# Relative-bias attention with a sine MLP on one core: the bias factors from matmuls instead of a pass through DRAM, and the first batch's values as casting loads

## The chip, the core and the metric

The kernel runs on one core of a Trainium2 chip. The core has a matrix engine (TensorE, PE in the profile, its weight loads PEld), a vector engine (VectorE, DVE), an engine for functions such as exp and sin (ScalarE, ACT), a general one (GpSimd, POOL) and one that mostly issues DMAs (SyncE, SP). Each has its own instruction stream and they meet through semaphores. SP, ACT and POOL can put loads into DMA queues; POOL's queue is called software_dynamic in the profile, that of SP and ACT hardware_dynamic. A load that changes the type from f32 to f16 on its way is called a casting load here; all of them are on POOL's queue. The metric is the time of one execution on the device in microseconds (us): before the change 375.01 us, the median of three runs (374.7 to 375.42).

## What is computed

Eight batches of attention with eight heads, 576 positions and head size 64, with a bias that depends on the distance of two positions alone; then an MLP on all 4608 rows with h + sin(alpha h)^2 / alpha as its function.

```python
scores = scale * np.matmul(q, k.transpose(0, 1, 3, 2))
bias = bias_table[bucket]                # bucket of |i - j|, 32 of them
scores = scores + bias.transpose(2, 0, 1)[None, :, :, :]
attn = np.exp(scores - np.max(scores, axis=-1, keepdims=True))
attn = attn / (np.sum(attn, axis=-1, keepdims=True) + 1e-09)
x = np.matmul(attn, v)                   # then to rows of 512
h = x @ w_in                             # 512 to 2048
s = np.sin(alpha * h)
out = (h + s * s / (alpha + 1e-09)) @ w_out
```

Buckets of all distances of 128 and more are the last one. The kernel uses exp(score + bias) = exp(score) times a factor, with the last bucket's bias taken off everywhere: the factor is then 1 outside a band of distances, and only blocks of the score matrix near the diagonal have to be multiplied. That band of factors, 384 wide for each head, is the tile `m2r` (with `mhr`, a smaller one for the last 64 keys of each head) before the change.

## The kernel before

**Stages.** For each batch t: keys and queries are brought to `kT` and `qT` (head dimension on partitions); TensorE makes scores for one pair of heads and 128 keys at a time (`qk` in `plan_unit`, kind A; kind C are the last 64 keys); ACT takes exp of them from PSUM into `u` (line 723); DVE multiplies by the band (lines 754 and 740); TensorE multiplies by the values `vs` and `vhs`, whose extra column of ones gives the row sum; DVE divides (lines 967, 968); the result goes to `xT`. Then come 16 steps f of the first MLP matmul, each with ACT's sin (1083), a square on ACT or DVE (1090, 1092) and DVE's sum (1097); the second MLP matmul (`w_out`) fills gaps of the next batch's attention.

**The first batch.** Its keys and queries come as plain or casting loads (`nat0` inside the tile natx, `nat1`), are cast on DVE and ACT (lines 488, 539, 540) and transposed on TensorE (`plan_tr`, lines 573 and 579); DVE copies the result to `kT` and `qT` (562). Its values come in f32 through SP's queue into a part of the `w_out16` tile (`load_v32`) and POOL casts them (`cast_v`). The band is made in `plan_table`: a small matmul takes the last bucket off the table, exp, a matmul with a constant 0/1 matrix phi spreads it over distances, ACT copies the 8 x 512 result to `e_sb`, which is written to DRAM (`e_dram`), and loads with one row's shift per partition read it back into `m2r` and `mhr`.

**The order of the work.** The instructions in the file's straight part (clears, first loads, seven matmuls on the zero tile `zz`) are issued in that order. All others are tasks of a planner (`Plan`), which simulates the five engines with the costs that each task names, picks the task that can start first (ties by priority), and emits the instructions in that order; `nb` is an earliest start that the code names for a task, and `HEAD_PRI` replaces the priority of some tasks by number. On each engine the chip then runs them in exactly that order. Where TensorE would have nothing to do in the first part, the planner puts in matmuls on `zz`. Waits are not written by hand: a layer below records what each instruction reads and writes, tile by tile, and makes the later instruction wait for the earlier one. POOL's loads take eight semaphores in turn.

**Lines that the text names.** `clear` (469 to 475) sets the parts of `kts`, `vhs` and `vs` that loads don't write, among them the column of ones of `vs` (475); for the first of two buffers it is called with DVE ahead of all casts, for the second with POOL.

Of the kernel before, what the change touches and what calls it, by code (L numbers as in the profile page):

```python
# [34 lines left out]
LAT = {"PE": 0.2, "ACT": 0.18, "DVE": 0.18, "POOL": 0.2, "SP": 2.4}  # L35
NBUF = {"ut": 2, "u": 2, "g": 2, "s16": 3, "sq": 3, "outs": 5, "xn": 6}
PAIRS = ((0, 1), (2, 3), (4, 5))
BANKS = {"h": (0, 1, 2, 3, 4, 5), "av": (6, 7), "mo": (7, 6)}

# [21 lines left out]
class Plan:  # L61
# [86 lines left out]
    def run(self, t0):  # L148
        free = dict(t0)
        todo = list(self.tasks)  # L150
        while todo:
# [21 lines left out]
            for e, c in cands.items():  # L173
                if not c:
                    continue
                s0 = min(x[0] for x in c)
                st, t = min(((x[0], x[1]) for x in c if x[0] <= s0 + SLACK[e]),
                            key=lambda x: (x[1].pri, x[0]))
                fin = st + t.engs[e]
                if best is None or (st, fin) < best[:2]:  # L180
                    best = (st, fin, e, t)
# [32 lines left out]
T_START = {"PE": 4.25, "ACT": 5.2, "DVE": 5.05, "POOL": 5.5, "SP": 5.0}  # L214
SPLIT = {0: 3, 1: 3}
PRI_S = 0
T_WI = 16.4
T_TAB = 4.9
T_PHI = 5.4
T_CL = 9.6  # L220
T_FIRST = (4.3, 5.35)
T_PAIR = ((7.05, 8.1), (8.9, 10.6), (12.5, 13.4))
PRI_TR = (350, 950, 1250)
T_VT = 9.7
T_ACT = ()
T_M2 = (12.4, 14.6, 16.0, 16.0)
T_MH = 13.5
T_RST = 20.0
T_WL = 25.0
T_V0 = (6.5, 8.8, 16.4, 16.9, 17.4, 17.9, 18.4, 18.9)  # L230
T_P3 = 8.3
# [5 lines left out]
T_LD = 33.0  # L237
# [4 lines left out]
SQ = {"ACT": 0.52, "DVE": 0.38}  # L242
T_V = ((15.0, 15.0), (53.5, 53.5))
T_TR1 = (35.5, 39.0)
T_W = (24.2, 27.0, 33.0, 33.0)
T_WO = (42.0, 45.0, 47.8, 51.0)
WARM0 = 7
WARM1 = 0
# [18 lines left out]
}  # L267
SIN_SET = "trig_and_small"
SLACK = {"PE": 0.02, "ACT": 0.02, "DVE": 0.02, "POOL": 0.02, "SP": 0.02}
# [14 lines left out]
def kernel(  # L284
# [26 lines left out]
    NE = 5  # L311
# [8 lines left out]
    e_dram = nc.dram_tensor("e_dram", [NE, 4 * H, EW], F16, kind="Internal")  # L320

    bt = _bucket_table(256)
    phi_np = np.zeros((NB, EW), dtype=np.float16)
    for x in range(EW - 1):
        phi_np[bt[abs(x - 255)], x] = 1.0
    last_np = np.eye(NB, dtype=np.float32)
    last_np[NB - 1] -= 1.0
    phi_h = nc.inline_tensor(phi_np, "phi_const")
    last_h = nc.inline_tensor(last_np, "last_const")
# [8 lines left out]
    m2r = sgl.tile([128, H, XW], F16, name="m2r")  # L338
    mhr = sgl.tile([128, NP, 192], F16, name="mhr")
    m2 = m2r[:, :, ::-1]  # L340
    mh = mhr[:, :, ::-1]
# [3 lines left out]
    vst = w_out16.rearrange("p f n -> p (f n)")[:, 0 : 2 * H * 4 * D].bitcast(F32).rearrange(  # L345
        "p (h c d) -> p h c d", h=H, c=4)
    vtt = w_out16.rearrange("p f n -> p (f n)")[:, 2 * H * 4 * D : 2 * H * 4 * D + 2 * NP * D].bitcast(
        F32).rearrange("p (h d) -> p h d", h=NP)
# [6 lines left out]
    tabE = sgl.tile([NB, H], F16, name="tabE")  # L355
    phi_sb = sgl.tile([NB, EW], F16, name="phi_sb")
    less_last = sgl.tile([NB, NB], F32, name="less_last")
    e_sb = sgl.tile([H, EW], F16, name="e_sb")
    alphaN = sgl.tile([NF, 128], F32, name="alphaN")
    idf_sb = sgl.tile([NF, NF], F32, name="idf_sb")  # L360
# [43 lines left out]

    def stage_kq(t):
        for dst, src in ((staged_k, k), (staged_q, q)):
            nc.gpsimd.dma_start(
                out=dst.ap()[t].rearrange("s (h d) -> s h d", h=H),
                in_=src[t].rearrange("h s d -> s h d"),
            )  # L410

    def load_kqT(t):
        nc.sync.dma_start_transpose(out=kTs[t % 2][:, :, :], in_=staged_k.ap()[t])
        nc.sync.dma_start_transpose(out=qTs[t % 2][:, :, :], in_=staged_q.ap()[t])

    def load_kt(t):
        for z in range(2):
            r = slice(64 * z, 64 * z + 64)
            nc.gpsimd.tensor_copy(out=kts[t % 2][r, :, r], in_=kTs[t % 2][r, :, 512:S])  # L419

    def load_v16(t):
        vp = v[t].rearrange("h s d -> s h d")
        for c in range(4):
            nc.gpsimd.dma_start(  # L424
                out=vs[t % 2][:, c, :, 0:D], in_=vp[128 * c : 128 * c + 128],
            )
        for z in range(2):
            load_vt(t, z)

    def load_v32(h):  # L430
        nc.sync.dma_start(out=vst[:, h], in_=v[0, h, 0:512].rearrange("(c p) d -> p c d", p=128))

    def load_vt32():
        vq = v[0].rearrange("(hp two) s d -> two s hp d", two=2)
        for z in range(2):
            nc.sync.dma_start(out=vtt[64 * z : 64 * z + 64], in_=vq[z, 512:S])

    def cast_vt():
        for z in range(2):
            r = slice(64 * z, 64 * z + 64)  # L440
            nc.gpsimd.tensor_copy(out=vhs[0][r, :, VC * z : VC * z + D], in_=vtt[r])

    def cast_v(h):
        nc.gpsimd.tensor_copy(out=vs[0][:, :, h, 0:D], in_=vst[:, h])
# [16 lines left out]
    def load_w_out16():  # L461
        src = moe_w_out.rearrange("(f p) n -> p f n", p=128)
        for fh in range(4):
            nc.gpsimd.dma_start(
                out=w_out16[:, 4 * fh : 4 * fh + 4, :], in_=src[:, 4 * fh : 4 * fh + 4, :]
            )

    def clear(eng, i):
        eng.memset(kts[i][0:64, :, 64:128], 0.0)
        eng.memset(kts[i][64:128, :, 0:64], 0.0)  # L470
        eng.memset(vhs[i][0:64, :, VC : 2 * VC], 0.0)
# [20 lines left out]
    def load_m2r(eng, h0, h1, r):  # L492

        eng.dma_start(
            out=m2r[:, h0:h1],
            in_=bass.AP(tensor=e_dram, offset=EW * (4 * H * r + h0), ap=[[1, 128], [EW, h1 - h0], [1, XW]]),
        )

    def load_mhr(eng):
        for z in range(2):  # L500
            eng.dma_start(  # L501
                out=mhr[64 * z : 64 * z + 64],
# [43 lines left out]
    def loads3():  # L546
        load_v16(1)
# [699 lines left out]
```

## Time and profile before

| | |
|---|---|
| median of three runs | 375.01 us |
| span of the profiled execution, first to last instruction | 372.5 us |
| what lies around the span, against the median | 2.5 us |
| busy share of PE, ACT, DVE, POOL | 98%, 85%, 69%, 24% |
| first cast of keys on DVE starts | 4.01 us |
| first exp on ACT starts | 9.39 us |
| first MLP matmul starts | 29.67 us |
| last idle time of PE over 0.3 us in the first 60 us ends | 52.40 us |

The page names lines of the kernel before. A row of the timeline is: start, time to the end of the last instruction of the row, engine, line, operation, tiles written and read, shape, count, and in brackets the engine's idle time before it with what ended it. A row of the windows is: stretch, its length, then busy time and count for PE, PEld, DVE, ACT and POOL, then the granted clock of TensorE, the DMA share and GB/s.

### The profile page before, as it was taken

The numbers are of one execution on the slowest core, as the hardware profiler recorded it, in microseconds if no ns is written. First come the engines' busy times: TensorE is split into PE (matmuls) and PEld (weight loads), VectorE is DVE, ScalarE is ACT, GpSimd is POOL, SyncE is SP. The second block draws the span as 40 slices with busy tenths as digits, with TensorE's granted clock in tenths as the row PEclk, the third lists the DMA queues.
The fourth block names the chain that finished last, engine by engine and source line by source line (L and its number), as shares of the span: only waits on it lengthen the run. The fifth ranks groups of instructions, "written<-read, shape, count | busy, mean of one in ns | idle before, by whom it ended". The sixth has DMA issues, their size and how long they took to land.

```text
span 372.5 us, 8907 instructions
## 1 busy us (share of the span) xinstructions
PE 363.7 (98%) x3563; PEld 195.3 (52%) x3563; DVE 258.8 (69%) x555; ACT 318.3 (85%) x436; POOL 89.2 (24%) x130
## 2 busy tenths in 40 slices
PE   6989989999999999999999999999999999999996
PEld 2455445644465445784554456444676455444443
DVE  4697966678776967597659866787669675879100
ACT  2898999989998999799989999899979997999211
POOL 5575360065000730064003700090006000000000
PEclk9599999999999999999999999999999999999999
DMA  9799999299824996199917992699249121000122
GB/s 167 152 191 208 203 170 155 61 146 123 113 60 99 115 151 112 48 161 138 135 48 135 126 169 59 115 114 171 60 111 118 65 58 48 7 18 13 59 85 84
DMA packets 149690, 40.69 MB, mean 109 GB/s; under 512 B 137144, under 2 KB 144656, under 8 KB 149648
## 3 DMA queue, kind: packets, MB, share of 16 engines
q0 software_dynamic: 94928, 17.47, 58.1%
q1 hardware_dynamic: 54352, 22.30, 25.5%
q8 instruction: 28, 0.46, 0.5%
q10 hardware_dynamic: 368, 0.34, 0.3%
q14 instruction: 14, 0.11, 0.1%
HBM read 37.73 MB, written 16.56 MB: 146 GB/s over the span
## 4 chain that ended last, share of the span: by engine, by line
PE 87%; DVE 4%; DMA 3%; ACT 3%; issue 1%; SPq 0%; ACTq 0%; DVEq 0%
PE pb L478 86%; DVE g L1097 1%; DMA tabN<-in_bias_table_dram 1%; DVE u L754 1%; DMA m2r<-e_dram 1%; DMA e_dram<-e_sb 1%; ACT sq L1090 1%; PE pb L1039 1%; ACT s L1083 1%; ACT nat L723 1%; DVE sq L1092 0%; DVE kT L562 0%; ACT L1161 0%; SPq L501 0%; DVE xn L968 0%
## 5 line engine op out<-in xcount | busy, mean ns | idle before, releaser
L723 ACT ACTIVATE u<-pb 128x1024 f16<-128x1024 f32 (+1 forms) x146 | 137.6, 1015 | 8.8 <-PE pb L478 7.4
L478 PE MATMUL pb<-w_out,g 128*128 128x512 f16 (+2 forms) x592 | 138.7, 374 | 0.5 <-DVE kT L562 0.5
L478 PE MATMUL pb<-xT,w_in 128*128 128x512 f16 (+4 forms) x704 | 127.5, 340 | 0.0
L1097 DVE SCALAR_TENSOR_TENSOR g<-sq,inv_a,pb 128x512 f16<-128x512 f16 x144 | 101.1, 743 | 7.7 <-ACT sq L1090 3.8
L1083 ACT ACTIVATE s<-pb,alphaT 128x512 f16<-128x512 f32 x144 | 92.9, 692 | 11.1 <-PE pb L478 10.2
L478 PEld LDWEIGHTS <-w_in 128*128 128x128 f16 x704 | 64.6, 98 | 57.1
L754 DVE TENSOR_TENSOR u<-u,m2r 128x768 f16<-128x768 f16 (+1 forms) x128 | 63.2, 498 | 35.6 <-ACT u L723 33.7
L478 PEld LDWEIGHTS <-g 128*128 128x128 f16 x592 | 54.0, 98 | 60.3 <-issue 5.4
L478 PEld LDWEIGHTS <-u 128*128 128x128 f16 x1152 | 43.1, 97 | 10.9 <-issue 5.8
L1090 ACT ACTIVATE sq<-s 128x512 f16<-128x512 f16 x75 | 46.8, 637 | 1.2 <-DVE g L1097 0.3
L419 POOL COPY kt<-kT 64x256 f16<-64x256 f16 x12 | 5.1, 428 | 174.2 <-DMA kT<-staged_k 144.9
L478 PE MATMUL pb<-qT,kT 64*128 64x64 f16 (+1 forms) x512 | 44.0, 293 | 1.6 <-ACT u L723 0.6
L478 PE MATMUL pb<-v,u 128*128 128x65 f16 x1024 | 43.7, 193 | 0.0
L1092 DVE TENSOR_TENSOR sq<-s 128x512 f16<-128x512 f16 x69 | 28.8, 427 | 12.1 <-ACT s L1083 11.2
L968 DVE TENSOR_TENSOR xn<-pb,rd 128x256 f16<-128x256 f32 (+2 forms) x59 | 28.5, 483 | 2.0
L478 PEld LDWEIGHTS <-kT 64*128 64x128 f16 x512 | 16.3, 95 | 23.1 <-issue 16.2
L478 PE MATMUL pb<-vh,u 128*128 128x130 f16 x128 | 28.3, 221 | 0.0
L424 POOL DMA_DIRECT2D v<-in_v_dram x28 | 24.8, 898 | 6.9 <-DMA w_in<-in_moe_w_in_dram 2.6
L560 ACT ACTIVATE outs<-pb 128x512 f32<-128x512 f32 (+2 forms) x10 | 5.5, 554 | 19.9 <-PE pb L478 19.9
L562 DVE COPY outs<-pb 128x512 f32<-128x512 f32 x27 | 18.5, 686 | 3.8 <-PE pb L478 3.8
L1161 ACT ACT_TABLE_LOAD x15 | 19.2, 1283 | 0.3
L967 DVE RECIPROCAL rd<-pb 128x4 f32<-128x4 f32 (+2 forms) x59 | 11.0, 186 | 10.8 <-PE pb L478 10.7
(74 smaller groups left out, 181.2 us busy)
## 6 DMA issues: line engine op xcount, KB each, us to landing
out_dram<-outs SPq DMA_DIRECT2D x35, 256.0 KB, 2.3
v<-in_v_dram POOLq DMA_DIRECT2D x28, 128.0 KB, 5.1
staged_k<-in_k_dram POOLq DMA_DIRECT2D x6, 576.0 KB, 9.6
staged_q<-in_q_dram POOLq DMA_DIRECT2D x6, 576.0 KB, 12.0
w_out<-in_moe_w_out_dram POOLq DMA_DIRECT2D x4, 512.0 KB, 17.4
w_out<-in_v_dram SPq DMA_DIRECT2D x8, 128.0 KB, 5.2
w_in<-in_moe_w_in_dram POOLq DMA_DIRECT2D x2, 512.0 KB, 6.3
w_in<-in_moe_w_in_dram POOLq DMA_DIRECT2D x1, 1024.0 KB, 11.6
```

What stands on the lines that cost most here:

```text
L424: nc.gpsimd.dma_start(out=vs[t % 2][:, c, :, 0:D], in_=vp[128 * c : 128 * c + 128],)
L478: nc.tensor.matmul(out=out, lhsT=lhsT, rhs=rhs, start=start, stop=stop)
L562: k_of(e).tensor_copy(out=o, in_=i)
L723: nc.scalar.activation(out=o, in_=x, func=AF.Exp, scale=0.125)
L754: nc.vector.tensor_tensor(out=io, in0=io, in1=m2[:, 2 * p : 2 * p + 2, x0 : x0 + hi - lo], op=ALU.mult)
L967: nc.vector.reciprocal(out=r, in_=x[:, :, :, D])
L968: nc.vector.tensor_tensor(out=xn[:, 0:n].rearrange("p c (z d) -> p c z d", z=2), in0=x[:, :, :, 0:D], in1=r.unsqueeze(3).to_broadcast([128 ...
L1083: nc.scalar.activation(out=s16.v, in_=h.v, func=AF.Sin, scale=alphaT[:, f : f + 1])
L1090: nc.scalar.activation(out=sq.v, in_=s16.v, func=AF.Square)
L1092: k_of(e).tensor_tensor(out=sq.v, in0=s16.v, in1=s16.v, op=ALU.mult)
L1097: nc.vector.scalar_tensor_tensor(out=gcell[b].v[:, f, :], in0=sq.v, scalar=inv_a[:, f : f + 1], in1=h.v, op0=ALU.mult, op1=ALU.add,)
L1161: nc.scalar.preload_act_table_set(name)
```

## The change

The band of factors is no longer written to DRAM and read back. The constant phi now has four shifted copies of the 32 buckets on its 128 partitions; `tab4` holds the table's exp, masked so that each of four columns sees one copy; 96 matmuls of 128 x 128 by 32 columns put the band into PSUM, and three copies (one on ACT, two on DVE) bring it to `m2`. `mh` is copied out of `m2`. The matrix that takes off the last bucket is computed from the identity on DVE instead of loaded. The bias table is the first load on POOL's queue.

The values of the first batch are casting loads on POOL's queue straight into `vs` and `vhs`; the loads through `w_out16` and POOL's casts are gone. All large loads are on POOL's queue in one order: `STATIC` in the straight part, then `LOADS`, w_in, the second batch's keys and queries, w_out, its values. The planner has a DMA engine of its own for them, and the named earliest starts of their users are replaced by dependences on these loads. The clears of both buffers are on DVE. `HEAD_PRI` has new numbers.

```diff
-T_PAIR = ((7.05, 8.1), (8.9, 10.6), (12.5, 13.4))
...
+STATIC = ((1, (1, 0)), (1, (1, 1)), (0, (0,)), (0, (1,)))
+LOADS = ((0, (2,)), (0, (3,)), (0, (4,)), (0, (5,)), (1, (2, 0)), (1, (2, 1)), (1, (3, 0)), (1, (3, 1)))
...
 HEAD_PRI = {
-    0: 3652.1, 1: 2400.7, 3: 2400.3, 4: 21.8, 5: 3600.9, 6: 3651.8, 7: 5849.8, 31: 5850.7, 32: -1199.3,
...
+    0: 3650.168307, 1: 10127.31486, 2: 3650.975104, 3: 3649.537641, 4: 3649.255957, 5: 3651.035224, 6: 3650.297449, 7: 6852.086188, 8: 3650.74746, 9: 10127.59543,
...
+    def load_v16c(t, c):
+        vp = v[t].rearrange("h s d -> s h d")
+        nc.gpsimd.dma_start(
+            out=vs[t % 2][:, c, :, 0:D], in_=vp[128 * c : 128 * c + 128],
+        )
...
-    def clear(eng, i):
+    def clear_k(eng, i):
         eng.memset(kts[i][0:64, :, 64:128], 0.0)
         eng.memset(kts[i][64:128, :, 0:64], 0.0)
+
+    def clear_v(eng, i):
         eng.memset(vhs[i][0:64, :, VC : 2 * VC], 0.0)
...
     P_ = nc.gpsimd
+    P_.dma_start(out=tabN, in_=bias_table)
     P_.memset(id_sb, 1.0)
...
+    P_.tensor_copy(out=idf_sb, in_=id_sb[0:NB, 0:NB])
...
+    for t, f in STATIC:
+        (load_kq1 if t else load_v0)(*f)
     nc.vector.memset(zz, 0.0)
-    clear(nc.vector, 0)
+    clear_v(nc.vector, 0)
+    clear_k(nc.vector, 0)
+    clear_k(nc.vector, 1)
+    nc.vector.tensor_scalar(
+        out=less_last, in0=idf_sb.unsqueeze(1).to_broadcast([NB, NJ, NB]),
+        scalar1=idf_sb[:, NB - 1 : NB], scalar2=None, op0=ALU.subtract
+    )
+    clear_v(nc.vector, 1)
     warm(WARM0)
...
-            load_m2r(nc.sync, 0, 2, 0)
-            load_mhr(nc.sync)
-            load_m2r(nc.sync, 2, 4, 3)
-            load_m2r(nc.sync, 4, H, 4)
-            for h in range(2, H):
-                load_v32(h)
...
+            def mm(e, b=b, w=w, s=0):
+                o = bank(b, 2).rearrange("p k x -> p (k x)")
+                for i in range(n // NJ // 2 * s, n // NJ // 2 * (s + 1)):
+                    x0 = EW - NJ - 128 - n * w - NJ * i
+                    full(o[:, NJ * H * i : NJ * H * (i + 1)], phi_sb[:, x0 : x0 + 128],
+                         tab4.rearrange("p h j -> p (h j)"), True, True)
...
+            x = plan.add({"PE": BAND_PE}, mm, [tab], -1100 + 10 * k, new=[b])
+            x = plan.add({"PE": BAND_PE}, lambda e, mm=mm: mm(e, s=1), [x], -1099 + 10 * k, use=[b])
+            bands[w] = plan.add({"ACT": 0.97, "DVE": 1.17}, cp, [x], -1098 + 10 * k, use=[b])
...
-        vt = plan.add({"POOL": 0.6}, lambda e: cast_vt(), [], 9003, nb=T_VT)
-        for h in range(H):
-            vdone.append(plan.add({"POOL": 0.45}, lambda e, h=h: cast_v(h), [], 9010 + h, nb=T_V0[h]))
...
+        for t, f in LOADS:
+            if t:
+                pool("n%d%d" % f, 0.63, lambda f=f: load_kq1(*f), 1.05)
+            else:
+                pool("u%d" % f, 0.88 if f[0] < 4 else 0.64, lambda f=f: load_v0(*f), 1.0 if f[0] < 4 else 0.3)
         for i, (x0, x1) in enumerate(((0, 1), (1, 2), (2, 4))):
...
+            pool("w%d" % i, 0.8, lambda x0=x0, x1=x1: load_w_in16(x0, x1), 2.8 * (x1 - x0))
```

What stands where is shown at three places; names ending in _49 are semaphores, DMASW0 to DMASW7 those of POOL's loads in turn, DMAHW those of SP's and ACT's.

The first is DVE at the start of the program, up to the cast of the first keys (natx). v_72 is the first buffer of `vs`, kt_70 and vh_74 those of `kts` and `vhs`; kt_71, vh_75 and v_73 the second ones. Before:

```order
L469 MEMSET kt_70 64x4x32
L470 MEMSET kt_70 64x4x32
L471 MEMSET vh_74 64x4x65
L472 MEMSET vh_74 64x4x65
L473 MEMSET vh_74 64x4
L474 MEMSET vh_74 64x4
L475 MEMSET v_72 128x32
L488 CAST natx<-natx 96x768 [waits DMAHW1_49,DMAHW0_49]
```

and now, from the same memset of v_72 on (the memsets of zz and vh_74 stand ahead of it):

```order
L485 MEMSET v_72 128x32 [waits DMASW4_49,DMASW3_49]
L477 MEMSET kt_70 64x4x32
L478 MEMSET kt_70 64x4x32
L477 MEMSET kt_71 64x4x32
L478 MEMSET kt_71 64x4x32
L532 TENSOR_SCALAR less_last<-idf_sb 32x128 [waits Pool_49]
L481 MEMSET vh_75 64x4x65
L482 MEMSET vh_75 64x4x65
L483 MEMSET vh_75 64x4
L484 MEMSET vh_75 64x4
L485 MEMSET v_73 128x32
L498 CAST natx<-natx 96x768 [waits DMAHW1_49,DMAHW0_49]
```

The memset of the ones' column of v_72 had no wait and now has one for two loads of POOL's queue; ten instructions stand between it and the cast.

The second is POOL's start, its first loads. Before (nat is the tile of the second to fourth pairs of heads, tabN the bias table, id_sb and idf_sb identities):

```order
L508 MEMSET id_sb 128x128
L509 ISA
L509 AFFINE_SELECT id_sb<-id_sb 128x128 [waits Pool_49]
L454 DMA nat_96<-in_k_dram 96x2x384
L454 DMA nat_96<-in_q_dram 96x2x384
L454 DMA nat_96<-in_k_dram 96x2x384
L454 DMA nat_96<-in_q_dram 96x2x384
L531 CAST idf_sb<-id_sb 16x16 [waits Pool_49]
```

and now:

```order
L503 DMA tabN<-in_bias_table_dram 32x8
L504 MEMSET id_sb 128x128
L505 ISA
L505 AFFINE_SELECT id_sb<-id_sb 128x128 [waits Pool_49]
L509 CAST idf_sb<-id_sb 32x32 [waits Pool_49]
L463 DMA nat_96<-in_k_dram 96x2x384
L463 DMA nat_96<-in_q_dram 96x2x384
L445 DMA v_72<-in_v_dram 128x8x64 x2
L445 DMA v_72<-in_v_dram 128x8x64 [waits DVE_49]
L445 DMA v_72<-in_v_dram 128x8x64
```

The table's load and the cast of the identity stand ahead of the loads; the fourth and fifth loads are the first two quarters of the values, and the third quarter waits for DVE.

The third is ACT around the first exp (u). Before:

```order
L540 ACTIVATE natx<-natx 96x6x64
L616 ACTIVATE tabE<-pb 32x8
L625 ACTIVATE e_sb<-pb 8x512
L626 DMA e_dram<-e_sb 8x5x512
L723 ACTIVATE u<-pb 128x2x512 x3
```

and now (m_76 is the tile m2):

```order
L543 ACTIVATE natx<-natx 96x6x64
L615 ACTIVATE tabE<-pb 128x8
L771 ACTIVATE u<-pb 128x2x512
L559 ACTIVATE m_76<-pb 128x8x128
L771 ACTIVATE u<-pb 128x2x512 x2
```

The copy and the write to DRAM ahead of the first exp are gone, and a copy of a third of the band stands behind it. On TensorE (not shown, its rows are long) the matmuls up to the first score matmul were: six transposes of keys, the table's matmul among four on zz, six transposes of queries, phi's matmul, six on zz. Now they are: six transposes of keys, three on zz, the table's matmul, six transposes of queries, three on zz, 16 of the band, 12 transposes of the second pair's keys, 16 of the band, 12 transposes of its queries.

More of the change, by code (lines that the diff above doesn't have):

```diff
@@ L423, in load_v16 @@
         for c in range(4):
-            nc.gpsimd.dma_start(
-                out=vs[t % 2][:, c, :, 0:D], in_=vp[128 * c : 128 * c + 128],
-            )
+            load_v16c(t, c)
         for z in range(2):
             load_vt(t, z)
[L430 to L444, printed above, removed]
     def load_vt(t, z):
@@ new lines, in plan_table, with half, load @@
+        for z in range(2):
+            def half(e, z=z):
+                r = slice(64 * z, 64 * z + 64)
+                k_of(e).tensor_copy(out=mh[r], in_=m2[r, z::2, 64 * z : 64 * z + 192])
+            bands["h%d" % z] = plan.add({"POOL": 0.95, "DVE": 0.37}, half, [bands[0], bands[1]], -1000 + z)
+    def load(eng, cost, emit, size, pri, deps=(), after=(), nb=0.0):
+        x = plan.add({eng: cost}, lambda e: emit(), deps, pri, nb, after=after)
+        y = x
+        if eng == "SP":
+            y = plan.add({}, None)
+            x.marks.append((y, cost - 2.2))
+            pri -= 1000
+        return x, plan.add({"DMA": size}, lambda e: None, [y], pri)
@@ L742, in bd @@
                 )
-            d = plan.add({"POOL": 0.6} if t == 0 and p else {"DVE": 0.25 if two else 0.15}, bd, [x],
-                         base + 10, nb=late, use=[ub])
+            d = plan.add({"POOL": 0.6} if t == 0 and p else {"DVE": 0.25 if two else 0.15}, bd, [x] + band,
+                         base + 10, use=[ub])
             for pp in (p, p + 1) if two else (p,):
```

288 lines of the change are left out of this document (150 added, 138 removed), and 37 rows, old and new, of the table HEAD_PRI.

## The prediction

> **What bounds the kernel now.** I read the page's busy times first, then the chain of waits, then windows cut where the head of the program changes its limit.
>
> ```profile
> span 372.5 us, 8907 instructions
> ...
> PE 363.7 (98%) x3563; PEld 195.3 (52%) x3563; DVE 258.8 (69%) x555; ACT 318.3 (85%) x436; POOL 89.2 (24%) x130
> ```
>
> ```profile
> 2.22 4.77 DMA tabN<-in_bias_table_dram
> ...
> 13.96 4.43 DMA m2r<-e_dram
> 18.48 1.61 DVE u L754 x3
> ...
> 52.40 2.60 PE pb L478 x44
> ```
>
> ```profile
> 0.00:9.39 9.39, 5.99 (x38) 2.62 (x40) 3.75 (x12) 2.56 (x4) 5.50 (x15) 0.94 0.91 167
> 9.39:29.67 20.28, 19.09 (x269) 11.20 (x270) 17.12 (x42) 18.73 (x25) 13.69 (x33) 0.78 0.97 175
> 29.67:52.40 22.73, 21.40 (x220) 10.39 (x217) 17.26 (x32) 21.67 (x36) 11.35 (x19) 1.00 1.39 199
> 52.40:312.00 259.60, 259.60 (x2721) 143.74 (x2721) 192.32 (x420) 240.16 (x313) 58.66 (x65) 1.00 0.95 110
> ```
>
> The chain names the DRAM pass of the band as the thing that is late in the head (the table lands at 6.99, the shifted band at 18.39, DVE multiplies from 18.48). The windows say where time can be won or lost at all: from 52.40 PE has no idle time for 260 us, so whatever the head does, the rest follows as a block, and the end moves by what PE's dense part moves. Ahead of it lie three stages: until the first exp at 9.39; until the first MLP matmul at 29.67, with ACT busy for 18.73 of 20.28 us; and until 52.40, where PE idles 22.73 − 21.40 = 1.33 us. The sum goes by these three.
>
> **The removed pass.** The band's way through DRAM leaves the head, but what it held up is not what bounds the second stage: ACT has 1.55 us without work there, and only that can be won while ACT's work is as long.
>
> **The first stage: a new wait on DVE.** This is the largest term. The memset of the ones' column of the values' first buffer now stands behind the first two loads into that buffer, in the code and so for the recording layer, and waits for their landing. Behind it on DVE stand ten instructions, and then the cast of the first keys, on which the transposes, the scores and the first exp hang. Before, DVE's start had no load ahead of that cast but the keys' own:
>
> ```profile
> 1.18 0.17 DVE L469 MEMSET kt<- 64x128 uint32 x1
> ...
> 1.66 0.28 DVE L471 MEMSET vh<- 64x260 f16 x1
> ...
> 2.70 0.09 DVE L475 MEMSET v<- 128x32 f16 x1 [0.16 <-issue]
> 4.01 0.56 DVE L488 CAST natx<-natx 96x768 f16<-96x768 f32 x1 [1.23 <-DMA natx<-in_k_dram]
> ...
> 10.01 0.76 DVE L562 COPY kT<-pb 128x576 f16<-128x576 f16 x1 [1.36 <-PE pb L579]
> ...
> 13.84 0.32 DVE L666 TENSOR_SCALAR tmp_a<-alphaT 128x16 f32<-128x16 f32 x1
> ```
>
> When the wait ends follows from POOL's issues. POOL's rows, and the landing times of the two kinds of load, the first for loads of keys and queries in the first 12 us, the second for whole quarters of values later on:
>
> ```profile
> 1.49 0.81 POOL L454 DMA_DIRECT2D nat<-in_k_dram  x1
> ...
> 3.54 0.64 POOL L454 DMA_DIRECT2D nat<-in_q_dram  x1
> 4.16 0.46 POOL L531 CAST idf_sb<-id_sb 16x16 f32<-16x16 f16 x1
> ```
>
> ```profile
> DMA to landing us min/median/max: 5.1/5.3/5.7
> ```
>
> ```profile
> L424 POOL DMA_DIRECT2D v<-in_v_dram x8: 893/898/905, 79.3 to 127.2; - x8
> ...
> DMA to landing us min/median/max: 3.6/5.6/6.5
> ```
>
> Before, the first key load was issued at 1.49. Now the table's issue (0.64, as other issues of POOL) and the identity's cast (0.46) come ahead of it: 2.59. The two loads of keys and queries take 0.64 each: 3.87. The first quarter of values takes 0.90: the second is issued at 4.77. It is a casting load in the same crowded stretch, so I take the head's 5.3 us: it lands at 10.1, between 8.4 (3.6) and 11.3 (6.5). The work behind the wait, by the distances of the starts above: 0.10 for the memset itself, two pairs on the keys' buffers, 0.48 each (1.18 to 1.66), 0.35 for the tensor_scalar (its row, with a shorter operand, and 0.03 to the next), the four of vh 1.04 (1.66 to 2.70), 0.10 for the second v buffer: 2.55 us. The first cast comes at about 12.6 in place of 4.01, **+8.5** (+6.8 to +9.8). POOL is held up too: its third quarter of values waits for that memset, and the second pair's keys stand behind POOL's copies of the first pair's. Those loads start late by the same shift, no more, and their users as well; I price that at nothing, with the head's own delay as the cover.
>
> By the Trainium skill ("DMA: Bandwidth & Descriptors", section "Anatomy of one DMA — SWDGE (gpsimd) path") a load of this path takes about 2.0 us plus its bytes at 436 GB/s, an estimate of 2.6 us for these 262 KB; the wait would end at 7.4 and the sum below would be lower by 2.7 us. No load in the rows above is that quick, so the rows stand.
>
> **From the cast to the first exp.** Before, 9.39 − 4.01 = 5.38 us, of which PE waited 1.94 for the table:
>
> ```profile
> 7.12 0.20 PE L478 MATMUL pb<-tabN,less_last 32*32 32x8 f32 x2 [1.94 <-DMA tabN<-in_bias_table_dram]
> ...
> 7.43 0.42 PE L573 MATMUL pb<-id_sb,natx 96*128 96x96 f16 x6
> ...
> 8.09 0.72 PE L478 MATMUL pb<-zz 128*128 128x128 f16 x6
> 8.74 0.61 PE L478 MATMUL pb<-qT,kT 64*128 64x512 f16 x2
> 9.28 0.69 PE L579 MATMUL pb<-id_sb,nat 96*64 96x96 f16 x12
> 9.90 0.61 PE L478 MATMUL pb<-qT,kT 64*128 64x512 f16 x2
> ...
> 19.18 0.41 PE L478 MATMUL pb<-v,u 128*128 128x65 f16 x8
> 19.43 0.22 PE L478 MATMUL pb<-vh,u 128*128 128x130 f16 x1
> ```
>
> That wait is gone, since everything has landed by 12.6. But PE now has, ahead of the first scores, the first pair's transposes, six matmuls on zz, 24 transposes of the second pair and 32 matmuls of the band. And its clock matters. Two stretches of before:
>
> ```profile
> 4.82:8.23 3.41, 1.47 (x22) 1.01 (x21) 1.34 (x3) 0.73 (x3) 1.66 (x4) 1.00 1.19 173
> 8.23:11.65 3.42, 3.42 (x38) 1.68 (x38) 1.65 (x3) 2.60 (x3) 0.71 (x3) 0.50 1.13 189
> ...
> 15.06:18.47 3.41, 3.41 (x35) 1.52 (x33) 2.89 (x6) 2.89 (x5) 1.94 (x9) 0.50 0.92 215
> 18.47:21.89 3.42, 2.68 (x36) 1.56 (x35) 3.38 (x8) 3.41 (x4) 1.94 (x5) 1.00 1.23 231
> ```
>
> After a stretch in which PE was busy for under half, the granted clock was 0.50 from 8.23 until 18.47, though PE worked all through it. Now PE ends its first seven zz matmuls at about 4.5 and idles until 12.6, so the half clock is there when the work begins. At that clock: cast 0.61; six transposes of natx twice, 2 × 0.62 (twice the 0.31 between the starts of six at full clock, estimated from the 0.42 of their row less one's lag of 0.11); two groups of three on zz, 2 × 0.33 (0.11 each, 8.09 to 8.74 for six); the table 0.13; 24 transposes of nat, 2 × 0.62 (9.28 to the next start at 9.90 for twelve); the score pair until ACT starts 0.65 (8.74 to 9.39): 4.5. The 32 band matmuls are of a form that the trace doesn't have, 128 weights and 32 columns. The nearest is v,u with 65 columns, 0.03 each at full clock (0.25 for eight, from 19.18 to the next start at 19.43); at half, 0.06: 1.9 us. From below 1.0 (full clock's 0.03), from above 3.5 (0.11, as zz with 128 columns at half clock). 4.5 + 1.9 = 6.4 in place of 5.38: **+1.0** (+0.1 to +2.6).
>
> The Trainium skill ("TensorE: Matmul & The Clock Gate", section "What's actually happening") has the full clock come back after a busy window of some 3.4 us. By that the head would leave half clock at about 16.6, worth an estimated 1.2 us on the sum. The rows above disagree (three such windows of full work at half clock); the first rival below prices the clock from rows.
>
> **The second stage.** ACT's exps are the same; it gains one copy of a third of the band and has idle time to lose:
>
> ```profile
> 9.39 2.18 ACT L723 ACTIVATE u<-pb 128x1024 f16<-128x1024 f32 x2 [0.61 <-PE pb L478]
> 11.75 3.61 ACT L723 ACTIVATE u<-pb 128x1024 f16<-128x1024 f32 x4 [0.17 <-PE pb L478]
> ...
> 15.87 8.65 ACT L723 ACTIVATE u<-pb 128x512 f16<-128x512 f32 x10 [0.52 <-PE pb L478]
> ```
>
> The copy has 1024 columns, as the exps of 0.9 have (3.61 for four): +0.9. Of 1.55 us idle I let 1.3 go, since the band is there before the first multiplication. DVE's two band copies, about 1.2 each (0.76 for a copy of 576 columns of PSUM, scaled), and the other 64 band matmuls lie beside ACT; DVE's 17.12 of 20.28 leave 3.2 us, which they use up nearly, so DVE could become the bound by a little. **−0.4** (±1).
>
> **The third stage.** The idle 1.33 us hang on the second batch's keys and queries:
>
> ```profile
> 47.00 0.45 PE L579 MATMUL pb<-id_sb,nat 96*64 96x96 f16 x12 [0.31 <-ACT qT L560]
> 47.91 0.59 PE L478 MATMUL pb<-w_out,g 128*128 128x512 f16 x2 [0.47 <-DVE kT L562]
> ...
> 52.40 0.67 PE L478 MATMUL pb<-qT,kT 64*128 64x512 f16 x4 [0.52 <-ACT nat L723]
> ```
>
> Their loads are issued by one queue without named starts, while their use is 8 us later; half of the idle time may go: **−0.6** (−1.3 to 0). After 52.40 the work is the same: nothing.
>
> **The sum.** 8.5 + 1.0 − 0.4 − 0.6 = +8.5 on a span of 372.5: 381.0. The median of the runs lies 2.5 us above this span, which I keep: **383.5 us**. A change of 0.2% is 0.75 us here, about what a measurement of this kernel can tell from none.
>
> **The rivals.** *The clock comes back early.* If the half clock ends while the head still makes its scores, the first stage's PE part halves: at full clock throughout, 24 + 12 transposes, zz and band fall from 5.2 to 2.6, about −2.8 with the score pair: 380.7; with one half window, 382.3. I take 381.5. For it speaks that the first seven matmuls keep PE busy for 3.17 of the first 4.4 us, against it the three half windows above. *The loads land fast.* With 3.6 us from issue to landing the wait ends at 8.4: 381.8. Against it: the head's loads lie within 5.1 to 5.7. *The band's matmuls are slow*, 0.11 each, with the half clock lasting into the second stage where 64 more of them stand between scores: +1.6 and about +1.4: 386.5. *The other side, faster:* the landing of the two loads holds nothing back, so that DVE casts at 4.01 as before. Then the removed table wait (1.94) pays against the band's 1.9, the second stage ends 0.5 to 1.5 earlier, the third loses its 0.6: 373. It decides if the wait ends by about 2 us, when DVE would have come to this memset; but the second of the loads is issued only at 4.77. So it needs the wait in the program to mean something else than the landing.
>
> **How the numbers follow.** Main case 383.5 (its own range 382 to 385) 0.50; early clock 0.20; fast loads 0.08; slow band 0.16; other side 0.05; no change 0.01. All but the last two are slower: slower 0.94, same 0.01, faster 0.05. The range takes in the bounds of the landing (−1.7, +1.2) and of the band's matmuls (−0.9, +1.6) about the cases: 379.5 to 387.5 leaves out the other side and the far ends, some 0.15.
>
> **What the profile after would show.** Right: DVE idle from about 2 to 10 us, ended by the load of v, at the memset of v's ones; the cast of natx at 12.6, the first exp at 19, the first MLP matmul at 38.8, PE dense from about 61. Wrong: if that idle time is short or ended by another load; if the granted clock is 1.00 in the 3.4 us after the first cast; if a band matmul takes far from 0.06; if w_out or the second batch's loads now end waits of PE between 45 and 65 us.

## The result, and the profile after

The changed kernel takes 380.99 us (median; 380.84 to 381.91) where the kernel before, measured beside it, takes 374.95: the ratio is 1.0163, with a 95% interval of 1.0142 to 1.0185. It is slower by 6.0 us, and the forecast of 383.5 (379.5 to 387.5) holds it.

The page of the changed kernel begins with

```profile
span 380.2 us, 9067 instructions
...
PE 365.0 (96%) x3662; PEld 199.9 (53%) x3662; DVE 267.4 (70%) x585; ACT 313.5 (82%) x428; POOL 87.8 (23%) x111
```

ACT has less work than before and PE hardly more; PE's share fell because the span grew. The windows, cut at the first exp, the first MLP matmul and the last idle time of PE, say where:

```profile
0.00:17.64 17.64, 8.90 (x94) 5.76 (x95) 6.72 (x25) 1.98 (x3) 8.55 (x19) 0.75 0.80 93
17.64:37.00 19.36, 17.20 (x313) 11.93 (x312) 18.34 (x46) 19.29 (x26) 13.76 (x21) 0.96 1.09 173
37.00:61.82 24.82, 23.75 (x241) 11.57 (x240) 20.87 (x44) 22.35 (x35) 8.62 (x9) 1.00 1.75 176
61.82:319.00 257.18, 257.18 (x2703) 142.89 (x2697) 192.11 (x421) 235.29 (x307) 56.92 (x64) 1.00 0.90 106
```

The first exp comes at 17.64 in place of 9.39 (+8.25), the first MLP matmul at 37.00 in place of 29.67 (+7.33). From 61.82 PE is busy without a break, and the last copy out on ACT, the end of the chain of waits, starts at 377.04 where it started at 369.69 (+7.35). After and before:

```profile
377.04 0.28 ACT outs L559
```

```profile
369.69 0.28 ACT outs L560
```

All of the loss is made ahead of the first exp, and 0.9 us of it is won back up to the first MLP matmul; after that nothing changes. These distances are of one execution of each kernel. Their spans lie 7.7 us apart and the medians only 6.0, so about 1.7 us of what the two traces show is spread from execution to execution.

What made the loss stands in DVE's timeline (all of its rows from the one before the wait to the cast, the like ones left out):

```profile
2.01 0.06 DVE L484 MEMSET vh<- 64x4 f16 x1
9.71 0.09 DVE L485 MEMSET v<- 128x32 f16 x1 [7.63 <-DMA v<-in_v_dram]
9.73 0.17 DVE L477 MEMSET kt<- 64x128 uint32 x1
...
11.81 0.58 DVE L498 CAST natx<-natx 96x768 f16<-96x768 f32 x1
```

and in the chain of waits, whose first long piece it is:

```profile
5.02 4.44 DMA v<-in_v_dram
...
9.71 0.09 DVE v L485
...
11.81 0.59 DVE natx L498
...
26.07 18.92 DMA w_out<-in_moe_w_out_dram
```

DVE stands still for 7.63 us at a memset of 0.09 us, until the second load of values has landed. PE pays with 7.48 us ahead of the first transposes. The row of w_out in the chain is new. It shows in PE's timeline as a wait which before had no like:

```profile
12.44 0.66 PE L572 MATMUL pb<-id_sb,natx 96*128 96x96 f16 x6 [7.48 <-DVE natx L498]
...
14.65 0.63 PE L488 MATMUL pb<-tab,phi_sb 128*128 128x32 f16 x16
15.21 0.69 PE L578 MATMUL pb<-id_sb,nat 96*64 96x96 f16 x12
...
45.03 0.38 PE L488 MATMUL pb<-w_out,g 128*128 128x512 f16 x1 [0.74 <-DMA w_out<-in_moe_w_out_dram]
```

### The profile page after: what moved, and what is told of

The parts are those of the page before. It is cut to its first block, busy times and chain, and to the rows that moved or that the text cites. A ratio compares the mean times of both kernels' runs of the same rounds, so it can differ in the third digit from the quotient of the medians.

```text
span 380.2 us, 9067 instructions
## 1 busy us (share of the span) xinstructions
PE 365.0 (96%) x3662; PEld 199.9 (53%) x3662; DVE 267.4 (70%) x585; ACT 313.5 (82%) x428; POOL 87.8 (23%) x111
## 4 chain that ended last, share of the span: by engine, by line
PE 87%; DMA 6%; DVE 3%; POOL 2%; issue 1%; ACT 0%; ACTq 0%; DVEq 0%; POOLq 0%
PE pb L488 86%; DMA w_out<-in_moe_w_out_dram 5%; DMA v<-in_v_dram 1%; POOL nat L463 1%; PE pb L578 1%; PE pb L1089 0%; DVE kT L561 0%; DVE g L1147 0%; PE pb L572 0%; DVE kt L601 0%; POOL v L445 0%; POOL kt L601 0%; DVE tmp_a L713 0%; DVE m L561 0%; ACT s L1133 0%
## 5 line engine op out<-in xcount | busy, mean ns | idle before, releaser
L803 DVE TENSOR_TENSOR u<-u,m 128x768 f16<-128x768 f16 (+1 forms) x128 | 62.0, 492 | 32.0 <-ACT u L771 30.1
L488 PEld LDWEIGHTS <-u 128*128 128x128 f16 x1152 | 44.1, 97 | 9.7 <-issue 3.5
L1140 ACT ACTIVATE sq<-s 128x512 f16<-128x512 f16 x73 | 45.7, 640 | 2.0 <-DVE g L1147 1.2
L488 PE MATMUL pb<-qT,kT 64*128 64x64 f16 (+1 forms) x512 | 42.1, 287 | 1.6 <-ACT u L771 1.4
L1142 DVE TENSOR_TENSOR sq<-s 128x512 f16<-128x512 f16 x71 | 29.6, 421 | 16.5 <-ACT s L1133 16.0
L445 POOL DMA_DIRECT2D v<-in_v_dram x32 | 28.4, 898 | 12.9 <-DVE v L485 4.2
L561 DVE COPY outs<-pb 128x512 f32<-128x512 f32 x29 | 19.9, 686 | 2.1 <-PE pb L488 1.9
L559 ACT ACTIVATE outs<-pb 128x512 f32<-128x512 f32 (+2 forms) x8 | 4.4, 544 | 19.8 <-PE pb L488 19.8
```

Of the source, the lines that this page charges most:

```text
L445: nc.gpsimd.dma_start(out=vs[t % 2][:, c, :, 0:D], in_=vp[128 * c : 128 * c + 128],)
L488: nc.tensor.matmul(out=out, lhsT=lhsT, rhs=rhs, start=start, stop=stop)
L561: k_of(e).tensor_copy(out=o, in_=i)
L803: nc.vector.tensor_tensor(out=io, in0=io, in1=m2[:, 2 * p : 2 * p + 2, x0 : x0 + hi - lo], op=ALU.mult)
L1140: nc.scalar.activation(out=sq.v, in_=s16.v, func=AF.Square)
L1142: k_of(e).tensor_tensor(out=sq.v, in0=s16.v, in1=s16.v, op=ALU.mult)
```

## The experiments

**The wait taken away.** The clear of the first buffer moves ahead of the loads, so that the loads wait for the memset (which is over long before they are issued) and not the memset for the loads. DVE's order is the same.

```diff
+    nc.vector.memset(zz, 0.0)
+    clear_v(nc.vector, 0)
     for t, f in STATIC:
         (load_kq1 if t else load_v0)(*f)
-    nc.vector.memset(zz, 0.0)
-    clear_v(nc.vector, 0)
```

> The changed kernel with one thing undone: DVE clears the first buffer of the values ahead of the loads into it, so that its memset waits for nothing and the loads wait for the memset. Theory (the wait at the head of DVE is what the change costs): DVE casts the first keys at about 4.2 us in place of 11.8, all that follows moves by about 7.6 us, 373.4 us (372.5 to 374.5), some 1.5 us better than the kernel before. Rival one (the one queue of loads is the bound and gives the gain back): the first MLP matmul moves from 37.0 to about 29.5, but PE then waits for w_out or the second batch's keys between 38 and 60, 376 to 379 us. Rival two (the band on TensorE and the order are what costs, the wait is hidden): 380 us or more.

Measured: 374.48 us, ratio to the kernel before 0.9977 (0.9953 to 1.0000). DVE, ACT and PE in its timeline:

```profile
4.33 0.57 DVE L498 CAST natx<-natx 96x768 f16<-96x768 f32 x1
```

```profile
10.12 1.02 ACT L771 ACTIVATE u<-pb 128x1024 f16<-128x1024 f32 x1 [3.44 <-PE pb L488]
```

```profile
29.11 0.81 PE L488 MATMUL pb<-xT,w_in 128*128 128x512 f16 x3
...
37.77 0.38 PE L488 MATMUL pb<-w_out,g 128*128 128x512 f16 x1 [1.37 <-DMA w_out<-in_moe_w_out_dram]
```

The cast comes 7.48 us earlier, the first exp 7.52, the first MLP matmul 7.89, and the ratio falls from 1.0163 to 0.9977, which is 7.0 us. The wait is the cause, and without it the rest of the change is worth little (the interval ends at 1.0000): the first MLP matmul is 0.56 us earlier than before the change, and PE then waits 1.37 us for w_out in place of 0.74. The first rival was right in its kind and too dear in its price.

**The wait put into the kernel before.** Two runs: the same two loads added behind the first pair of keys and queries that POOL loads, which is the second pair of heads (into the second batch's buffer, which is loaded again later), and then the same with a memset of that buffer on DVE ahead of the first cast.

```diff
     load_pair(1)
+    for c in range(2):
+        nc.gpsimd.dma_start(out=vs[1][:, c, :, 0:D],
+            in_=v[1].rearrange("h s d -> s h d")[128 * c : 128 * c + 128])
     load_pair(2)
...
     clear(nc.vector, 0)
+    nc.vector.memset(vs[1][:, :, :, D : D + 1], 1.0)   # second run alone
```

> The kernel before with two more casting loads on POOL's queue behind the first pair's keys and queries: the first two quarters of the second batch's values into their buffer (loaded again later, as before). Nothing waits for them. It is the control of the run with a wait. Theory (a wait costs, traffic hardly): the second and third pairs' loads are issued 1.8 us later, 375.5 us (375 to 376.5). Rival (the traffic of values in the head's first 10 us costs by itself): first exp and first MLP matmul later by 2 us or more, 377 to 379 us.

> As the kernel before with two more loads of values, and DVE sets the ones' column of that buffer behind its other clears, ahead of the cast of the first keys: one memset more, which waits for both loads, as in the changed kernel. Theory: the wait ends at 8.3 to 9.1 us (second load issued at 3.8), DVE's cast of the first keys comes at about 8.7 in place of 4.0, and all of it goes through to the end: 4 to 5.5 us above the run without the wait, 379 to 381 us. Rival (the band's way through DRAM hides DVE's wait, since it ends at 18.4 anyway): less than 2 us above it.

Measured: 376.88 us (ratio 1.0033, 1.0011 to 1.0055) with the loads and 381.86 (1.0147, 1.0096 to 1.0199) with the wait as well. DVE's cast in the first and in the second run:

```profile
4.16 0.95 DVE L488 CAST natx<-natx 96x768 f16<-96x768 f32 x1 [1.38 <-DMA natx<-in_k_dram]
```

```profile
11.11 0.56 DVE L488 CAST natx<-natx 96x768 f16<-96x768 f32 x1 [8.33 <-DMA w_out<-in_v_dram]
```

One memset that waits makes the cast 6.95 us later, and of that 5.0 us by the medians, 4.3 by the ratios, reach the end. The second row names a load into w_out's tile, which landed at the same time (11.09); this cast doesn't read that tile. The memset ahead of the cast waits for the two added loads, the second issued at 3.8, and their landing took up to 7.1 us, longer than expected; why is not shown. The loads alone cost more than expected too: the first exp comes at 9.47, but the first MLP matmul at 32.41, 2.7 us later than before. The rival that the band's pass through DRAM would cover it falls. What absorbed the other 2 us is in PE's waits, in the run with the loads alone

```profile
PE pb L478 <- DVE kT L567: 1.9, 2, 1.4
...
PE pb L478 <- DMA tabN<-in_bias_table_dram: 0.5, 1, 0.5
```

and in the run with the wait, where the table has landed and of the waits for kT 0.5 us are left:

```profile
PE pb L478 <- DVE kT L568: 0.5, 1, 0.5
```

**The clock.** 32 more matmuls on the zero tile, so that PE has no idle time ahead of its first transposes in the changed kernel.

```diff
-WARM0 = 7
+WARM0 = 39
```

> The changed kernel, with 39 in place of 7 matmuls on the zero tile at the start, so that PE is busy from 1.3 to about 12 us and doesn't idle ahead of its first transposes. Theory (PE's idle time ahead of the first work puts the head's matmuls at half clock, as the prediction has it): granted clock 1.00 from 12 to 15 us at least, the way from the first cast to the first exp falls from 5.8 to 3.5 to 4.5 us, 379 us (378.2 to 379.8). Rival (the transposes bring the half clock anyway, or the head is bound by DVE's copies): first exp within 0.5 us of 17.6, 381 us (380.5 to 381.5).

Measured: 380.96 us, ratio 1.0133 (1.0091 to 1.0174); the interval overlaps that of the changed kernel (1.0142 to 1.0185), so no gain at the end is shown. In its timelines:

```profile
16.28 1.02 ACT L771 ACTIVATE u<-pb 128x1024 f16<-128x1024 f32 x1 [2.44 <-PE pb L488]
```

```profile
14.12 0.55 PE L488 MATMUL pb<-tab,phi_sb 128*128 128x32 f16 x16
14.60 0.45 PE L578 MATMUL pb<-id_sb,nat 96*64 96x96 f16 x12
...
35.27 0.81 PE L488 MATMUL pb<-xT,w_in 128*128 128x512 f16 x3
...
44.52 0.38 PE L488 MATMUL pb<-w_out,g 128*128 128x512 f16 x1 [1.96 <-DMA w_out<-in_moe_w_out_dram]
```

Twelve transposes take 0.38 us (14.60 to the next start, 14.98) in place of 0.63 (15.21 to 15.84), the way from the cast (12.03) to the first exp is 4.25 in place of 5.83, and the first MLP matmul comes 1.73 us earlier. But the first w_out matmul starts only 0.51 us earlier: the load is not there, and the wait for it grew from 0.74 to 1.96. In these two executions the last copy out starts 0.55 us earlier (376.49). The half clock is real and is worth 1.6 us up to the first exp; the wait for the load takes most of it back. Neither theory had this.

**The loads behind the wait.** The order of loads is the next suspect: the first quarter of w_out goes ahead of the second batch's keys and queries in the queue, every other engine's order being the same.

```diff
-                pool("kq%d" % kq, 0.8, lambda kq=kq: load_nat2(kq), 3.1)
+                pool("kq%d" % kq, 0.8, lambda kq=kq: load_nat2(0) if kq else load_w_out16(0), 3.1)
...
-            wq.append(("wo%d" % f, 0.76, lambda f=f: load_w_out16(f), 2.65))
+            wq.append(("wo%d" % f, 0.76, lambda f=f: load_w_out16(f) if f else load_nat2(1), 2.65))
```

It was run with the wait taken away, with the longer row on the zero tile, and on the changed kernel as it is.

> The run with the clear ahead of the loads, and the first quarter of w_out loaded ahead of the second batch's keys and queries in the one queue, in place of behind them. Theory (the queue of loads took part of the head's gain back: PE waited 1.4 us for w_out at 37.8): that wait is gone, 373.1 us (372.5 to 373.9) where the run with the clear alone had 374.5, and 1.5 to 2.5 us below the kernel before. Rival (the queue is full, so another load is late in its stead): PE waits for the second batch's keys or queries from 40 on, 374 to 375 us.

> The run with the longer row of matmuls on the zero tile, and the first quarter of w_out ahead of the second batch's keys and queries. Theory (the full clock brought the first exp 1.4 us forward, and PE's wait for w_out, 2.0 us there in place of 0.7, gave it back): with w_out early both show, 379 us (378.4 to 379.6), and 1 to 1.5 us below the changed kernel with w_out first alone. Rival (the clock's gain is lost elsewhere, between the first exp and the first MLP matmul): equal to the changed kernel with w_out first within 0.5 us.

> The changed kernel with the first quarter of w_out ahead of the second batch's keys and queries, and nothing else. It is the control of the two others. Theory: PE's wait of 0.7 us at 45.0 is gone and no other comes: 380.3 us (379.8 to 380.8). Rival (another load is late in its stead): 381 us or more.

Measured: 374.06 us (ratio 0.9985, 0.9963 to 1.0008), 382.44 (1.0188, 1.0149 to 1.0226) and 381.52 (1.0177, 1.0146 to 1.0208). The wait for w_out is gone in all three, but nothing that shows is won, and all three lie above what was expected. In the first of them the profile shows a new wait of PE, for DVE, and behind it two copies of 64 by 64 elements that take nine and twelve times as long as their likes. The chain of waits, POOL's timeline and PE's:

```profile
45.18 1.64 DVE kt L601
...
46.84 2.21 DVE kt L601
...
49.06 1.42 DVE g L1147 x2
```

```profile
44.61 2.21 POOL L419 DMA_DIRECT2D staged_k<-in_k_dram  x1 [2.53 <-DMA w_out<-in_moe_w_out_dram]
46.57 2.47 POOL L419 DMA_DIRECT2D staged_q<-in_q_dram  x1
```

```profile
49.86 0.39 PE L488 MATMUL pb<-qT,kT 64*128 64x64 f16 x15 [2.49 <-DVE g L1147]
```

DVE's first copy ends at 46.82, when POOL's issue of the first large load ends; the second starts then and ends at 49.05, when the second issue ends (49.04). Elsewhere the same copy takes 0.18 us. So DVE's small copies between two SBUF tiles waited for POOL while POOL issued. POOL's two issues are not earlier than in the version with the clear alone (44.61 for 43.74); the copies are. Without the wait for w_out DVE comes to them at 45.18 in place of 47.32 and meets both issues, where it met only the end of the second, for 0.85 us. The other two versions show the same kind of wait of PE for DVE, 1.4 and 0.4 us. The execution shown took 376.86 us, 2.8 over the median of its kernel, so its 2.49 us of wait are more than is usual there.

**The copies moved off DVE.** The first pair of such copies of the second batch goes to ACT, behind ACT's own copy of the same keys; run with w_out first, with w_out where it was, and beside the former run with w_out first once more.

```diff
+                if t == 1 and e == "DVE" and moved in ([], [p]):
+                    moved[:] = [p]
+                    nc.scalar.activation(out=kts[t][r, p, r], in_=kTs[t][r, p, 512:S], func=AF.Copy)
+                    continue
                 k_of(e).tensor_copy(
```

> The run with the clear ahead and w_out first, and the two small copies into the second batch's kt that DVE held for 1.6 and 2.2 us while POOL issued two large loads are done on ACT, behind its own copy of the same keys. Theory (DVE's copies wait for POOL while it issues; they are what gave w_out's gain back): no DVE instruction of 64x64 takes over 0.3 us, PE's wait of 2.5 us at 49.9 is gone, and the median falls by 0.5 to 1.5 us against the run with w_out first in the same call: 372.6 to 373.6 us. Rival (ACT's two copies more are as late for the scores as DVE's were): within 0.4 us of it.

> The run with the clear ahead of the loads, with the same two small copies on ACT, w_out where it was. Theory: DVE's copies were held 0.7 us there, off the path while PE has other work, and PE's wait of 1.4 us for w_out stays: within 0.5 us of the run with the clear alone, 374 to 374.8 us, and above the run with both. Rival (the copies alone were what cost): 373.5 us or less.

> The run with the clear ahead and w_out first once more, as the control of the run with the copies on ACT on the same chip: 373.7 to 374.5 us. In its profile DVE's two small copies at 45 to 49 us are long wherever they meet POOL's two large issues.

Measured, in that order: 373.17 us (ratio 0.9962, 0.9938 to 0.9987), 374.06 (0.9979, 0.9955 to 1.0003) and 373.89 (0.9980, 0.9956 to 1.0003). With w_out first the medians with and without the copies on ACT lie 0.7 us apart, but the intervals overlap, so a gain is likely and not settled. ACT's two take 0.52 us together, and PE's longest wait between 40 and 55 us is short:

```profile
46.47 0.52 ACT L604 ACTIVATE kt<-kT 64x64 f16<-64x64 f16 x2
```

```profile
52.39 0.25 PE L488 MATMUL pb<-vh,nat 128*64 128x130 f16 x2 [0.23 <-DVE qT L562]
```

In the control the copies took 2.34 us and PE waited 0.97 for DVE. Of the 2.0 us between the ends of the two profiled executions (last copy out at 367.81 and 369.79) 0.8 are there at the first MLP matmul, 28.51 and 29.35, ahead of any of these copies. With w_out where it was the copies on ACT gave 374.06, as expected no more than the run without the wait had, but not in the expected way: its profile has no wait for w_out. There PE waited 1.28 us at 14.2 for a load of keys, transposes from 16.62 on ran at half rate (0.62 us for twelve), and the first MLP matmul came at 30.25, late enough for w_out to have landed. So a load was late there too, but another one. One more expectation was wrong: another pair of copies on DVE still takes 0.77 us where it meets the second issue, so it is not so that none takes over 0.3. The first of the three is the one version whose interval lies below the kernel before: 0.4% faster.

The same two mendings with the wait left in and the longer row on the zero tile (its edits stand above):

> The changed kernel with its wait left in, with the longer row of matmuls on the zero tile, w_out first and the two small copies on ACT. Theory (the full clock is worth 1.4 to 2 us at the first MLP matmul and was given back first to w_out, then to DVE's two copies held by POOL): with both out of the way PE has no wait over 0.6 us between 36 and 62 us, and the time is 379 to 380.2 us, 1 to 2 us below the changed kernel. Rival (the gain goes elsewhere each time, since the loads or ACT bound this stretch): 380.5 us or more, with a new wait of PE in it.

Measured: 379.90 us, ratio 1.0130 (1.0080 to 1.0180). PE's waits:

```profile
PE pb L488 <- ACT u L776: 1.5, 4, 0.5
...
PE pb L488 <- DVE qT L562: 0.2, 1, 0.2
```

No new one stands between 36 and 62 us, and the time lies in the expected range, 1.1 us below the changed kernel. The intervals overlap, and by its ratio this version can't be told from the longer row alone (1.0133), so a gain from the two mendings is not shown by the times. In the traces, one execution each, the last copy out starts at 374.80, 1.7 us before that of the longer row alone; they show the gain given back to these two waits.

**The loads of values alone.** In the kernel before, the first batch's values as four casting loads on POOL's queue behind the third pair of keys and queries that POOL loads, two more for the last rows; the loads through w_out's tile and POOL's casts are gone.

```diff
     def load_v32(h):
-        nc.sync.dma_start(out=vst[:, h], in_=v[0, h, 0:512].rearrange("(c p) d -> p c d", p=128))
+        return
...
     def cast_v(h):
-        nc.gpsimd.tensor_copy(out=vs[0][:, :, h, 0:D], in_=vst[:, h])
+        pass
...
     def load_pair(p):
...
+        if p == 3:
+            for c in range(4):
+                P_.dma_start(out=vs[0][:, c, :, 0:D],
+                    in_=v[0].rearrange("h s d -> s h d")[128 * c : 128 * c + 128])
```

> The kernel before with the values of the first batch as casting loads on POOL's queue, behind the third pair's keys and queries, into buffers that DVE has cleared; the loads through w_out's tile and POOL's ten casts are gone. The band still goes through DRAM. Theory (as such the new loads of values are worth nothing, since POOL's casts hid beside other work): 375 us (374.5 to 376), first MLP matmul at 29.2 to 30.7. Rival (POOL's casts were what held the loads of w_in and w_out): 373 to 374.3 us. Other rival (the values land too late for the first matmul that uses them at 19): 376 to 379 us.

Measured: 375.39 us, ratio 1.0015 (0.9986 to 1.0045): no difference that shows. The first MLP matmul of its profiled execution (376.43 us, 1.0 over the median) comes at 31.75, 2.1 us later than before and later than expected; how far that belongs to this placing of the loads, the run does not tell. So the small gain of the version without the wait is not to be had from the loads of values alone in this place; the band was not tried alone.

## Why the prediction was right, and where its terms were off

**The wait at the head of DVE: right, +7.8 for +8.5.** The landing took 4.4 us (3.7 to 4.6 over the head's loads of values), nearer the quick end than the 5.3 taken from the loads of keys; the wait ended at 9.7 for 10.1. The work behind it took 2.10 us for 2.55: the distances of the rows before the change included waits for issue, and the last memset of the ten doesn't stand in the cast's way (its row starts at 11.92, the cast's at 11.81).

**From the cast to the first exp: right in kind, +0.45 for +1.0.** The half clock came (0.50 from 11.65 to 18.47), with the second pair's transposes at the price taken (0.63 us for twelve). The first pair's were cheaper (0.46 for 0.62, twice) and the table's matmul dearer (0.53 for 0.13), which nearly cancel. The 32 band matmuls ahead of the scores were mis-sized: 16 take 0.56 us to the next start (14.65 to 15.21), 0.035 each and not 0.06. They hardly follow the clock, since at full clock 16 take 0.48 (14.12 to 14.60 in the run with the longer row). Doubling the full-clock price of the nearest row was the step that failed; the lower bound held.

**The second stage: −0.9 for −0.4.** ACT was busy for 19.29 of 19.36 us: 1.48 of its 1.55 us of idle time went, where 1.3 were taken, and its work grew by 0.56 for 0.9.

**The third stage: 0.0 for −0.6; this step failed in its mechanism.** The three idle times that the prediction shows did go, but the loads did not come early enough for a new need, and PE's idle time only fell from 1.33 to 1.07 us. The planner now uses w_out at 45.03, 8 us after the first MLP matmul, where it used it 18 us after it. PE waits for w_out, whose 18.92 us from issue to landing (the row of the chain) are no longer hidden. The prediction named such a wait as what would show it wrong, and it gave it no price.

The terms sum to +7.35 at the last copy out, for +8.5. The last store is 0.35 longer in the profiled execution. That execution took 381.91 us, 0.9 over the median of its kernel, and only 1.7 us lay around its span, where the prediction kept 2.5. These two, which have nothing to do with the change, are the greater part of the 2.5 us by which the forecast was too high. What was kept for the time around the span was mis-sized: in every later execution of the kernel before 1.7 to 1.8 us lie around the span, so the span of 372.5 was that of an execution of about 374.2, quicker than the median of 375.01. The forecast span of 381.0 came within 0.8 us of the profiled one, and part of that is luck: the errors of the terms have both signs.

**The rivals.** The early clock would have been worth 1.6 us at the first exp (not 2.8) and nothing that shows at the end. The fast landing was nearly half true. The slow band was wrong by its price. The other side needed the memset not to hold DVE; the version where it doesn't got 374.48 and not 373. PE's wait of 1.37 us for w_out is part of that; how much of it is not settled, since w_out first alone won nothing that shows.

## What to carry to other kernels

In a layer that tracks whole tiles, as here, a memset into a tile whose loads are issued ahead of it waits for those loads, even where they write other columns (7.63 us here); when such a clear stands in an in-order engine's head, price everything behind it, and put the clear first in the program. When an experiment speeds up the head and the end doesn't move, look for the next late thing at once and mend it together with the first: here, by the traces, time went to a load, and then to small copies that met a DMA issue. Don't read a gain of a microsecond from one profiled execution of each kernel. Price a new narrow matmul between bounds and don't scale it with the clock.

## What the runs showed of the hardware

**DVE copies wait for POOL's issues.** The copies of 64 by 64 f16 between SBUF tiles took 0.18 us alone and 1.64 and 2.21 us when POOL issued loads of 2.21 and 2.47 us, each ending within 0.02 us of the issue's end. Not all of DVE's work is held: in the version with the copies on ACT a square at 46.25 us, inside POOL's second issue (45.81 to 48.27), took 0.42 us as elsewhere. The Trainium skill ("SBUF — State Buffer", section "SBUF: two separate sides") has DVE and GpSimd share a pair of ports as an exclusive lock: whichever starts first holds it for its whole instruction, and the other blocks; its warning is of POOL's DMAs that wait for DVE. The trace agrees with such a lock, with DVE as the one that waits, until the end of the issue; that the ports are the reason it can't show.

**The granted clock of the record is not always the rate of the matmuls.** In the version without the wait the window and PE's rows in it read

```profile
4.82:8.23 3.41, 3.41 (x50) 3.01 (x48) 2.68 (x7) 0.70 (x2) 3.41 (x5) 1.00 1.40 136
```

```profile
7.74 0.69 PE L578 MATMUL pb<-id_sb,nat 96*64 96x96 f16 x12
8.36 0.61 PE L488 MATMUL pb<-tab,phi_sb 128*128 128x32 f16 x16
```

and the kernel before with two loads more shows 1.00 from 4.82 to 18.47. Yet twelve transposes take 0.62 us in both, as they do at a granted 0.50, and 0.38 in the run with the longer row. In the first 20 us the duration of a known matmul tells the rate, and the column alone doesn't.

When the full rate comes differs between executions with the same order on PE up to the first exp. In the version without the wait PE works from 1.26 on and the half rate lasts until about 9.5. With w_out first and the copies on ACT, PE starts as early, and its first transposes of the second pair are already at full rate:

```profile
7.27 0.45 PE L579 MATMUL pb<-id_sb,nat 96*64 96x96 f16 x12
```

Twelve take 0.38 us there (the next start is 7.65). In the five profiled executions of such versions the full rate comes between about 4 and 9.5 us and the first exp between 8.53 and 10.12. By the Trainium skill ("TensorE: Matmul & The Clock Gate", section "What's actually happening") the full rate comes after some 3.4 us of busy PE, and where in a free-running window the work starts matters; four of the five come near that, with about 3 to 5 us of work, and the version without the wait, with 8, differs.
